# Two layers of Infini-attention and FFN: the order of each engine's operations as a written list of turns

## The chip, the cores and the metric

The kernel runs on one core of a Trainium2 chip. A core has five engines that each work through a list of instructions of their own: TensorE (PE) for matmuls, VectorE (DVE), ScalarE (ACT) and GpSimd (POOL) for everything elementwise, and SyncE (SP), which here only issues DMA transfers. Semaphores tie the lists together: an instruction can wait until another engine or a transfer has counted a semaphore up to a value. Matmul results land in PSUM, 8 banks of 512 floats for each of 128 partitions, and have to be moved from there to SBUF by DVE or ACT before the bank can be used again.

The metric is the device time of one execution in microseconds. The profile was taken from one execution of its own.

## The reference

The input x has 2048 tokens of 640 features, all in bf16. The stack is attention, FFN, attention, FFN, with the same weights for both rounds and a layer norm without parameters ahead of each part:

```python
x = x + A(layernorm(x), wq, wk, wv, wo, beta)
x = x + B(layernorm(x), w1, w2)      # relu(x @ w1) @ w2, 1728 hidden units
x = x + A(...)
x = x + B(...)
```

A is attention with a memory. 32 heads of 20 features work on 4 segments of 512 tokens. For every segment s and head:

```python
logits = qs @ ks.T * scale + mask            # causal, within the segment
a_dot  = softmax(logits) @ vs
a_mem  = (phi(qs) @ M) / (phi(qs) @ z + 1e-6)
o      = g * a_mem + (1 - g) * a_dot         # g = sigmoid(beta), one per head
M      = M + phi(ks).T @ vs                  # phi(t) = t + 1 if t > 0 else exp(t)
z      = z + phi(ks).sum(0)
```

The segments' outputs are put together and multiplied by wo.

## The kernel before

**Tiles and stages.** A segment of 512 tokens is the unit of all work, so there are 8 (round, segment) pairs. For each, four token tiles of 128 are normalised (DVE writes them to xn_tok, L704, or L716 in the first segment and in the FFN's norm), turned by a transposing DMA, and projected on PE: q and k with the features on the partitions (groups of 5 matmuls; the first of a group is recorded at L651, the others at L654), v with the tokens on the partitions. DVE or ACT moves each result out of its bank: q and k to the staging tile stg (DVE L827, ACT L828), v to v_aug, which has a column of ones for the denominators (DVE L878, ACT L879). q and k of two groups of 4 heads go through DRAM (scr) to pad, where each head begins at a multiple of 32 partitions, so that four heads' scores can be computed side by side in row tiles of PE (L1114, "rows"). ACT takes the exp of the scores into PT (L1166), POOL clears what lies above the diagonal (L1178), and PE multiplies by v in column tiles (L1257, "cols"), 16 matmuls with one evacuation to av (DVE L1265, ACT L1266); a DMA turns av to avt, and DVE divides by the sums (L1293, L1294, L1301). For two of the 32 pairs of head groups (all segments and rounds together) the product is formed by token instead, with the division straight from the bank (L1220, L1221, L1224).

The memory runs beside this: phi is a max (DVE L967), an exp (ACT L974) and a min (DVE L975); the update of M is PE L1058, the read PE L1007, always into the first of four banks, with its division on DVE (L1015, L1017, L1018), which frees that bank with L1018. The sum of both parts is turned and multiplied by wo, and DVE adds the result to x (L1328), which frees the bank and feeds the statistics of the next norm (L662, L664, L672). The FFN's first matmuls write hT (ACT L1436, DVE L1434), a last narrow part of the hidden units runs in column tiles (L1405), and its second matmuls are added to x at L1328 as well.

**Banks.** Four of the eight banks hold scores. The other four (MISC) are shared by all else that PE computes, so every evacuation by DVE or ACT sets when a later group of matmuls can start.

**What sets the order.** `plan()` describes the work as 33 streams, generators that yield one operation after another, each with the engines that may run it, a modelled duration, and the operations that it waits for. They are named by the order in which they are added: a is the scores, b the exps, d the products with v, h and i the projections by wo, j and k the FFN's norms, l and m the transfers to pad and scr, q and r the memory reads, y and z the projections to k and q, A that to v, B the FFN, E the constants (among them beta_bc), F the first loads. `Sched.run` simulates the engines: at each step it looks at the head of each stream, works out when it could start by the model, and takes the one with the earliest start, by priority where several tie. What it takes goes to the end of that engine's list. `keep_busy` puts small matmuls on the identity (L638) into PE's list where it expects a gap. SWITCH_NS, what it charges for a change of PE's mode, is varied over 48 values (STARTS), and of the 48 plans the one with the smallest sum of `late()` is taken, a replay of the plan with random delays of transfers. For these inputs that is the plan for 79.0. `Prog` leaves out waits that follow from earlier ones, and `emit` writes the lists.

So an operation's place in its engine's list is fixed when the kernel is built, and on the chip each engine works strictly in that order: an instruction that waits holds up all behind it on its engine.

## Time and profile before

| | |
|---|---|
| median of 3 runs | 562.49 us (562.12 to 563.04) |
| the profiled execution | 562.46 us |
| its span in the trace | 560.6 us |
| granted clock of PE | 1.00 |
| busy | PE 99%, DVE 73%, ACT 73%, POOL 35%; weight loads 54% |
| DMA engines, packets of queue 1 | 45.7% |

The span begins with the first instruction and ends with the last; the profiled execution's own time is 1.86 us longer. Lines such as L1265 are lines of the kernel before. In the timeline, consecutive instructions of one line on one engine are one row, with start and length in microseconds and their count behind the x; lengths of pipelined instructions overlap, so the distance between two starts tells more than the length. Square brackets at the end of a row hold idle time ahead of it and who ended it.

### The profile page before, as it was taken

Reading aid. Unit: us, or ns where it says so; the run is one execution under the profiler, and the core shown is the slowest. Engines: PE = TensorE matmul, PEld = TensorE weight load, DVE = VectorE, ACT = ScalarE, POOL = GpSimd, SP = SyncE. Lnnn points to the kernel's source line nnn. Section 1 sums busy time; section 2 is a strip of 40 time slices with the busy share of each in tenths; the row PEclk is TensorE's granted clock in tenths of the full one; section 3 lists DMA queues with packets and bytes.
Section 4 is the critical chain, followed back from the end, with each engine's and each line's share of the span. In section 5 each row is a group of like instructions: output and inputs, shape, how many; then the busy total and the mean of one; then the engine's idle time right before and its main releaser. Section 6 shows DMA issues by size and latency. Waiting matters only on the chain.

```text
span 560.6 us, 12651 instructions
## 1 busy us (share of the span) xinstructions
PE 555.5 (99%) x5110; PEld 302.6 (54%) x5111; DVE 410.8 (73%) x1060; ACT 409.7 (73%) x522; POOL 194.3 (35%) x302
## 2 busy tenths in 40 slices
...
DMA packets 132219, 61.43 MB, mean 110 GB/s; under 512 B 111042, under 2 KB 122050, under 8 KB 132162
## 3 DMA queue, kind: packets, MB, share of 16 engines
q1 hardware_dynamic: 131942, 60.37, 45.7%
...
q10 hardware_dynamic: 220, 0.26, 0.2%
q14 instruction: 17, 0.14, 0.1%
...
## 4 chain that ended last, share of the span: by engine, by line
PE 90%; DVE 8%; DMA 1%; ACT 0%; POOL 0%; issue 0%
PE ps L654 58%; PE ps L651 12%; PE ps L1114 9%; PE ps L1257 7%; DVE stats L662 2%; PE ps L1058 2%; PE ps L1007 2%; DVE x_sb L1328 1%; PE ps L1405 1%; DVE stg L827 1%; DMA x_sb<-in_A_x_dram 1%; DVE xn_tok L704 1%; DVE av L1265 0%; DVE xn_tok L716 0%; DVE mv L664 0%; ACT PT L1166 0%
## 5 line engine op out<-in xcount | busy, mean ns | idle before, releaser
L1166 ACT ACTIVATE PT<-ps 128x1024 bf16<-128x1024 f32 x320 | 310.1, 1022 | 66.1 <-PE ps L1114 64.5
L1178 POOL TENSOR_SCALAR_AFFINE_SELECT PT<-PT 128x512 bf16<-128x512 bf16 x256 | 166.3, 668 | 267.7 <-ACT PT L1166 267.7
L654 PE MATMUL ps<-w_r,hT 128*128 128x320 bf16 (+2 forms) x768 | 123.4, 299 | 0.1
L654 PE MATMUL ps<-xnT,w_r 128*128 128x512 bf16 x416 | 113.6, 379 | 0.0
L1328 DVE TENSOR_TENSOR x_sb<-x_sb,ps 128x320 bf16<-128x320 bf16 (+1 forms) x128 | 60.4, 479 | 70.2 <-PE ps L654 69.9
L654 PEld LDWEIGHTS ps<-w_r,hT 128*128 128x128 bf16 x768 | 72.2, 98 | 34.2 <-issue 6.3
L1436 ACT ACTIVATE hT<-ps 128x512 bf16<-128x512 f32 x55 | 33.0, 599 | 46.4 <-PE ps L654 46.1
L1114 PE MATMUL ps<-pad 20*128 20x384 bf16 (+3 forms) x1024 | 64.9, 301 | 0.0
L654 PEld LDWEIGHTS ps<-xnT,w_r 128*128 128x128 bf16 x416 | 39.7, 98 | 42.1 <-issue 2.9
L662 DVE BATCH_NORM_STATS2 stats<-x_sb 128x6 f32<-128x320 bf16 x126 | 55.9, 470 | 2.3 <-DMA x_sb<-in_A_x_dram 2.0
L1265 DVE CAST av<-ps 128x512 bf16<-128x512 f32 x56 | 38.3, 684 | 12.9 <-PE ps L1257 12.5
L1114 PEld LDWEIGHTS ps<-pad 20*128 20x128 bf16 x1024 | 18.2, 92 | 51.4 <-ACT PT L1166 24.2
L654 PE MATMUL ps<-wo_r,oT 128*128 128x320 bf16 x256 | 45.3, 299 | 0.0
L1434 DVE TENSOR_SCALAR hT<-ps 128x512 bf16<-128x512 f32 x49 | 33.5, 684 | 10.5 <-PE ps L654 10.0
L1257 PE MATMUL ps<-PT,v_aug 128*32 128x256 bf16 (+5 forms) x896 | 40.7, 302 | 0.0
L651 PE MATMUL ps<-xnT,w_r 128*128 128x512 bf16 x104 | 39.6, 381 | 0.0
L654 PE MATMUL ps<-wv_r,xnT 128*128 128x320 bf16 x192 | 35.8, 300 | 0.0
L654 PE MATMUL ps<-xnT,wk_r 128*128 128x512 bf16 (+1 forms) x140 | 35.5, 349 | 0.0
L676 POOL TENSOR_TENSOR rstd<-lnU,mhalf 128x2 f32<-128x2 f32 (+2 forms) x25 | 20.3, 811 | 39.9 <-DVE lnU L672 39.7
L654 PE MATMUL ps<-xnT,wq_r 128*128 128x512 bf16 (+1 forms) x140 | 33.9, 349 | 0.0
L1301 DVE TENSOR_TENSOR o_sb<-avt,rden 128x320 bf16<-128x320 bf16 x60 | 33.3, 572 | 0.7
L654 PEld LDWEIGHTS ps<-wo_r,oT 128*128 128x128 bf16 x256 | 24.8, 98 | 11.3 <-issue 1.3
...
## 6 DMA issues: line engine op xcount, KB each, us to landing
...
```

The lines of the kernel that those rows point to most:

```text
L651: bk, tk = yield pe(mm_ns(n), [(lambda e, bk, a=a, b=b: e.matmul(bk.ap[:, 0:n] if len(b.shape) == 2 else bk.ap[:, 0:n].rearrange("p (i n) ...
L654: tk = yield pe(mm_ns(n), [(lambda e, k=k, a=a, b=b, bk=bk: e.matmul(bk.ap[:, 0:n] if len(b.shape) == 2 else bk.ap[:, 0:n].rearrange("p (i ...
L662: tk = yield dve(320, 1, lambda e, c2=c2: e.bn_stats(stats6[:, t, c2, :], x_sb[:, t, c2 * 320:(c2 + 1) * 320]), xt)
L1114: fns.append([(lambda e, z=z, j=j, hh=hh, N=N, o=o, sl=sl: e.matmul(ps[:, hh, o:o + N], sl.ap[32 * hh:32 * hh + DH, z, 0, 128 * j:128 * j ...
L1166: tx = yield act(1024, lambda e, dst=dst, src=src: e.activation(dst, src, ACT.Exp, scale=SCALE), sc + pw)
L1178: tm = yield pool(600.0, lambda e, reg=reg: e.affine_select(out=reg, in_=reg, pattern=[[0, 4], [1, 128]], compare_op=ALU.is_ge, fill=0.0, ...
L1257: fns.append((lambda e, bk, j=j, hh=hh, pt=pt, g=g0 + z: e.matmul(bk.ap[32 * hh:32 * hh + wide(g, hh), 128 * j:L], VAUG[vx(a, s)][:, j].re ...
L1265: te = yield evac(L, 1, lambda e, sl=sl, z=z, bk=bk: e.tensor_copy(sl.ap[:, z], bk.ap), lambda e, sl=sl, z=z, bk=bk: e.activation(sl.ap[:, ...
L1301: to = yield dve(320, 1, lambda e, dst=dst, src=src, rz=rz: e.tensor_tensor(dst, src, rz, ALU.mult), [tg] + OSB.tks)
L1328: ta = yield dve(n, 1, lambda e: e.tensor_tensor(x_sb[:, t, c0:c0 + n], x_sb[:, t, c0:c0 + n], bk.ap[:, 0:n], ALU.add), [tk] + list(waits) ...
L1434: th = yield evac(512, 1, lambda e, dc=dc, bk=bk: e.tensor_scalar(hT[:, dc, :], bk.ap[:, :], 0.0, None, ALU.max), lambda e, dc=dc, bk=bk: ...
L1436: lambda e, dc=dc, bk=bk: e.activation(hT[:, dc, :], bk.ap[:, :], ACT.Relu), [tk] + HT.tks)
```

## The change

STARTS holds the single value 79.0, whose plan is the one that was taken before. `Sched` now also records each operation that it places. TURNS holds, for each of the five engines, a string with one letter per operation: the stream whose turn it is. `in_turns` builds a second `Prog` from the record: on each engine it takes the next operation of the stream named, so that a stream keeps its own order on that engine while streams pass each other, with the same engines, buffers and dependencies as in the plan, and works out anew which waits have to be written. That `Prog` is emitted. The letter H stands for the small matmuls of `keep_busy`.

On PE 2006 of 5113 operations stand at another place than before (by at most 40 places), on DVE 783 of 1062 (16), on ACT 92 of 526 (9), on SP 261 of 324 (15), on POOL 45 of 306. Lines in the new file are numbered 107 higher from `Sched`'s methods on, so that L1265 is L1372 there.

```diff
-STARTS = [SWITCH_NS + 0.75 * (k - 48 // 2) for k in range(48)]
+STARTS = [79.0]
...
+TURNS = {
+    "sp": (
+        "FFEFFFFFFFllllllmGmwwllllGmGGsGmllleGlllslGGGmGwwmemslGGGllmmGGGlllllslllllmGGggwwGllmmmmGGGelGljksG"
...
         self.log = []
+        self.record = []
...
+            fns = [(lambda e, ap=s.ap: self.idle_fn(e, ap), False)] * n
+            for fn, mark in fns:
+                self.P.op("pe", fn, mark)
+            self.record.append(("pe", len(self.streams), fns, None, s.tks, [], s, "full", 56.0 * n))
...
             self.log.append((e, hold, tail, waits, out if isinstance(out, list) else [out], op.dma is not None))
+            self.record.append((e, best[0][2], fns, op.dma, waits, out if isinstance(out, list) else [out], slot, op.mode, op.alts[k][1]))
...
+    def in_turns(self, turns):
+
+        names = "abcdefghijklmnopqrstuvwxyzABCDEFGHIJKLMNOPQRSTUVWXYZ"
+        todo = {e: {} for e in ENGS}
+        for r in self.record:
+            todo[r[0]].setdefault(names[r[1]], []).append(r)
+        seq = {e: [r for r in self.record if r[0] == e] for e in ENGS}
+        for e, order in turns.items():
+            assert sorted(order) == sorted(n for n, rs in todo[e].items() for _ in rs), e
+            its = {n: iter(rs) for n, rs in todo[e].items()}
+            seq[e] = [next(its[n]) for n in order]
+        P = Prog(self.P.clk)
...
+                    P.waits(e, [new[t] for t in waits])
+                    if sem is not None:
+                        got = [P.dma(e, fns[0][0], sem)]
+                    else:
+                        got = [t for t in [P.op(e, fn, mark) for fn, mark in fns] if t is not None]
...
+        P.waits("sp", [new[id(self.last[0]), self.last[1]]])
+        return P
...
-            S.P.emit(block)
+            S.in_turns(TURNS).emit(block)
```

Three places in the lists. The first is on DVE, at about 98 us of the trace, around the division of a memory read (rmem, om_sb) and the evacuation of a product with v (av). Before:

```order
L716 TENSOR_SCALAR xn_tok<-x_sb,mv,rstd 128x640 x2
L1015 TENSOR_SCALAR rmem<-ps 128x16
L975 TENSOR_TENSOR stg<-stg,rtmp 128x512
L967 TENSOR_SCALAR rtmp<-stg 128x512
L1017 RECIPROCAL rmem<-rmem 128x16
L1018 TENSOR_TENSOR om_sb<-ps,rmem 128x320
L1265 CAST av<-ps 128x512
```

After, at the same place on DVE:

```order
L1122 TENSOR_SCALAR rmem<-ps 128x16
L1124 RECIPROCAL rmem<-rmem 128x16
L1125 TENSOR_TENSOR om_sb<-ps,rmem 128x320
L1372 CAST av<-ps 128x512
L1082 TENSOR_TENSOR stg<-stg,rtmp 128x512
L1074 TENSOR_SCALAR rtmp<-stg 128x512
```

The min and the max of phi (stg, rtmp) moved behind the division and the evacuation.

The second is SP's list at the start: the loads of x, of the weights (wk_r, wq_r, wv_r) and of beta_bc, and the first transfers to pad. Before:

```order
L524 DMA x_sb<-in_A_x_dram 128x640
L518 DMA x_sb<-in_A_x_dram 128x2x640
L521 DMA wk_r<-in_A_wk_dram 128x5x256
L521 DMA wq_r<-in_A_wq_dram 128x5x256
L521 DMA wk_r<-in_A_wk_dram 128x5x384
L521 DMA wq_r<-in_A_wq_dram 128x5x384
L511 DMA wv_r<-in_A_wv_dram 128x5x640
L518 DMA x_sb<-in_A_x_dram 128x2x640 x2
L924 DMA pad<-stg 20x1024 x4
L610 DMA beta_bc<-in_A_beta_dram 128x32
```

After, on SP from the first row:

```order
L631 DMA x_sb<-in_A_x_dram 128x640
L625 DMA x_sb<-in_A_x_dram 128x2x640
L717 DMA beta_bc<-in_A_beta_dram 128x32
L628 DMA wk_r<-in_A_wk_dram 128x5x256
L628 DMA wq_r<-in_A_wq_dram 128x5x256
```

The load of beta_bc moved from behind the pads to the third place, and the other loads of weights follow in their old order.

The third is on DVE again, at about 314 to 318 us, where xn_tok is written for the next norm and results of wo are added to x_sb. Before:

```order
L704 TENSOR_SCALAR xn_tok<-x_sb,mv,rstd 128x640 x3
L1328 TENSOR_TENSOR x_sb<-x_sb,ps 128x320 x2
L704 TENSOR_SCALAR xn_tok<-x_sb,mv,rstd 128x640
L662 BN_STATS stats<-x_sb 128x6 x2
L1015 TENSOR_SCALAR rmem<-ps 128x16
```

After, at the same place on DVE:

```order
L811 TENSOR_SCALAR xn_tok<-x_sb,mv,rstd 128x640 x4
L1435 TENSOR_TENSOR x_sb<-x_sb,ps 128x320 x2
L1122 TENSOR_SCALAR rmem<-ps 128x16
L769 BN_STATS stats<-x_sb 128x6 x2
L1400 RECIPROCAL rden<-avt 128x32
```

The fourth write of xn_tok moved ahead of the two additions.

80 lines of the change are left out of this document (78 added, 2 removed).

## The prediction

> **What bounds the kernel now.** I read the page's first two lines, then the chain that ended last, then the timeline of PE, and last what the other engines do where PE stands still.
>
> ```profile
> span 560.6 us, 12651 instructions
> PE 555.5 (99%) x5110; PEld 302.6 (54%) x5111; DVE 410.8 (73%) x1060; ACT 409.7 (73%) x522; POOL 194.3 (35%) x302
> ```
>
> PE is busy for 555.5 of 560.6 us, so all idle time of PE together is 5.1 us, and some of that is the wait for the first data. A busy PE might still be slow, so the second question is its cadence. Three pieces of the chain (start, us, engine, line, count) show it where nothing disturbs:
>
> ```profile
> 489.15 1.76 PE ps L654 x13
> ...
> 504.63 0.86 PE ps L654 x4
> ```
>
> Thirteen matmuls of 320 columns take 1.76 us, 0.136 us each; four of 512 columns take 0.86, 0.216 each. In the timeline the durations of single matmuls overlap, so I work with starts: a stall is the distance between two starts less the count times this cadence. A change of order doesn't change these two numbers. It can only change the places where PE leaves the cadence, and there are two kinds.
>
> The first kind is a change of PE's mode (whole array, row tiles for the scores at L1114, column tiles for L1257 and L1405). The timeline (start, us, engine, line, operation, tiles, count) at one scores round:
>
> ```profile
> 128.66 0.57 PE L654 MATMUL ps<-w_r,hT 128*128 128x320 bf16 x3
> 129.16 0.40 PE L1114 MATMUL ps<-pad 20*128 20x512 bf16 x4
> 129.49 1.40 PE L654 MATMUL ps<-w_r,hT 128*128 128x320 bf16 x9
> ```
>
> Three matmuls should take 0.41, and the scores start after 0.50: 0.09 lost. Four scores matmuls lie side by side and should take 0.216; PE goes on after 0.33: 0.11 lost. So a change of mode costs 0.10. Counted along PE's list of operations there are 404 of them, some 40 us.
>
> The second kind is a wait. The largest of them, and what DVE did there:
>
> ```profile
> 99.20 0.71 PE L654 MATMUL ps<-wv_r,xnT 128*128 128x320 bf16 x4
> 99.87 0.34 PE L1007 MATMUL ps<-BD,w_r 128*128 128x147 bf16 x3
> 100.47 0.31 PE L651 MATMUL ps<-wv_r,xnT 128*128 128x320 bf16 x1 [0.25 <-DVE av L1265]
> ```
>
> ```profile
> 98.51 0.41 DVE L975 TENSOR_TENSOR stg<-stg,rtmp 128x512 bf16<-128x512 bf16 x1
> 98.84 0.28 DVE L967 TENSOR_SCALAR rtmp<-stg 128x512 bf16<-128x512 bf16 x1
> 99.04 0.24 DVE L1017 RECIPROCAL rmem<-rmem 128x16 f32<-128x16 f32 x1
> 99.32 0.49 DVE L1018 TENSOR_TENSOR om_sb<-ps,rmem 128x320 bf16<-128x320 f32 x1
> 99.73 0.68 DVE L1265 CAST av<-ps 128x512 bf16<-128x512 f32 x1
> ```
>
> The four matmuls from 99.20 end their turn at 99.74, but L1007 starts at 99.87, when L1018 has emptied the only bank that L1007 may use: 0.13. Its three matmuls take 0.19 (no wait is near them where I measured that), and L651 starts at 100.47 instead of 100.05, when L1265 has emptied its bank: 0.42. Together 0.54 us. Smaller ones stand at 58.86,
>
> ```profile
> 58.33 0.57 PE L654 MATMUL ps<-wv_r,hT 128*128 128x320 bf16 x3
> 58.86 0.84 PE L1058 MATMUL ps<-v_aug,phk 128*128 128x147 bf16 x10
> ```
>
> at 324.64,
>
> ```profile
> 324.17 0.38 PE L654 MATMUL ps<-xnT,w_r 128*128 128x512 bf16 x1
> 324.64 0.29 PE L638 MATMUL ps<-ident 128*128 128x128 bf16 x2
> ```
>
> and at 390.24:
>
> ```profile
> 389.99 0.30 PE L654 MATMUL ps<-w_u,hL 128*128 128x320 bf16 x1
> 390.24 0.34 PE L1007 MATMUL ps<-BD,stg 128*128 128x147 bf16 x3
> ```
>
> By the same reckoning 0.12 at 58.86 (0.53 less 0.41), 0.25 at 324.64 (0.47 less 0.22) and 0.11 at 390.24 (0.25 less 0.14). Two more, at 78.5 and 94.9, are about 0.10 each. This is nearly all that PE waits for once it has started: little more than 1.2 us can be won from waits.
>
> **The change, part by part.** Both kernels hold the same operations, buffers and choices of engine; the order in each engine's list is all that differs, with the waits that the order makes explicit.
>
> *Waits that go.* At 98.5 to 100.3 the new turns put L975 and L967 behind L1017, L1018 and L1265. From the starts above, these two take 0.53 us of DVE (98.51 to 99.04), so the bank of L1018 is free 0.53 earlier and that of L1265 as well: more than the 0.13 and the 0.42 that PE waits. Both stalls go: 0.54. At 58.86 the emptying of a bank (L1220, L1221, L1224) moves ahead of two multiplications L1301, each longer than the wait: 0.12. At 324.64 the release is this evacuation:
>
> ```profile
> 324.15 0.44 DVE L878 CAST v_aug<-ps 128x320 bf16<-128x320 f32 x1
> ```
>
> It moves ahead of three DVE operations, and the stall of 0.25 goes. The three of about 0.10 go likewise: 0.30. Sum of waits: 0.54 + 0.12 + 0.25 + 0.30 = 1.21 us. What is late next at these places is the matmul before, so nothing takes their place there.
>
> *Changes of mode.* The new PE list has 400 instead of 404: 4 x 0.10 = 0.40 us.
>
> *New waits on DVE.* This is the price I know least. PE owns few banks, so a DVE operation that moves ahead of an evacuation hands its own length to PE, as far as the margin doesn't cover it. The clearest case is here, first DVE and then PE:
>
> ```profile
> 315.29 0.87 DVE L1328 TENSOR_TENSOR x_sb<-x_sb,ps 128x320 bf16<-128x320 bf16 x2
> 316.09 0.43 DVE L704 TENSOR_SCALAR xn_tok<-x_sb,mv,rstd 128x640 bf16<-128x640 bf16 x1
> 316.44 0.87 DVE L662 BATCH_NORM_STATS2 stats<-x_sb 128x6 f32<-128x320 bf16 x2
> ```
>
> ```profile
> 316.02 0.30 PE L651 MATMUL ps<-wo_r,oT 128*128 128x320 bf16 x1
> ```
>
> L704 (316.09 to 316.44, so 0.35) now stands ahead of the pair L1328. The first of the pair ends in the middle, near 315.7, and frees the bank for the L651 at 316.02; 0.35 later is past 316.02 with what a wait needs, and I put PE's wait at 0.15. DVE can't make this up, since it has no gaps there. The stretch (length, then busy time of PE, PEld, DVE, ACT, POOL, PE clock, DMA share, GB/s):
>
> ```profile
> 310.00:327.00 17.00, 16.91 (x178) 9.20 (x176) 16.84 (x51) 13.65 (x16) 8.40 (x12) 1.00 0.39 83
> ```
>
> Comparing for each wait of PE on DVE how much work has moved ahead on DVE with the time to spare in the trace, I find 17 places where more was moved than was spare, the first and the last being the L651 of these two rows:
>
> ```profile
> 26.56 0.28 PE L651 MATMUL ps<-xnT,wq_r 128*128 128x256 bf16 x1
> ```
>
> ```profile
> 498.98 0.30 PE L651 MATMUL ps<-wo_r,oT 128*128 128x320 bf16 x1
> ```
>
> Of these I followed seven operation by operation. Five cost nothing, since DVE idles just before and the moved work falls into the gap; one costs 0.15, the one above, and one 0.10. So 0.25 for seven, 0.036 a place, and 17 x 0.036 = 0.6 us. The bounds: nothing, if all margins hold, and 0.35 (one L704) at half of the places, 9 x 0.35 = 3.15 us.
>
> *The start.* SP now issues the load of beta_bc third, ahead of all weights, instead of after the first pads. The two issues (start, us), the two transfers (KB, us to landing), the DMA engines' stretch, and the first use of wv:
>
> ```profile
> 4.63 2.12 SPq L511 DMA_DIRECT2D wv_r<-in_A_wv_dram  x1
> ...
> 17.52 0.49 SPq L610 DMA_DIRECT2D beta_bc<-in_A_beta_dram  x1
> ```
>
> ```profile
> wv_r<-in_A_wv_dram SPq DMA_DIRECT2D x1, 800.0 KB, 8.8
> ...
> beta_bc<-in_A_beta_dram SPq DMA_DIRECT2D x1, 8.0 KB, 2.6
> ```
>
> ```profile
> 2.00:13.00 11.00, 10.45 (x107) 9.40 (x106) 5.78 (x20) 5.69 (x13) 4.37 (x6) 1.00 1.04 330
> ```
>
> ```profile
> 14.07 0.30 PE L651 MATMUL ps<-wv_r,xnT 128*128 128x320 bf16 x1
> ```
>
> wv lands at 4.63 + 8.8 = 13.43 and is first used at 14.07; in the new PE list three matmuls of 256 columns (0.109 each, by the cadence of the others) fewer stand ahead, so it is wanted at 13.75, and 0.32 is to spare. If the queue is what counts, wv's issue slips by beta's 0.49 and PE waits 0.17. If the transfers count, for they are at their limit (share 1.04), 8 KB at 330 GB/s are 0.02 us and it's hidden. At worst all 2.6 us of beta's flight are added: 2.3 of wait. I take 0.1, between the two near ones. wk, wq and x are wanted at least two microseconds after they land. On DVE the small memset of the warm-up tile moves into the chain of the first layer norm:
>
> ```profile
> 1.77 0.06 DVE L580 MEMSET warm<- 128x1 f32 x1
> ```
>
> DVE works without a gap there until PE can start, so it costs its 0.06.
>
> *ACT, POOL and SP.* On ACT, 92 of 526 operations move; the largest single ones put an exp of phi ahead of a pair of softmax exps. It falls into time that ACT waits anyway (in total, times, longest), 0.58 us on average, as long as one such exp:
>
> ```profile
> ACT PT L1166 <- PE ps L1114: 64.5, 111, 2.4
> ```
>
> POOL is busy 35% of the time, and its 45 moved operations I put at nothing: the cover is its idle time. SP's later moves (transposes earlier, spills later) reach operations that are wanted a microsecond or more after they land; if that cover were gone, each would cost its delay, a few tenths.
>
> **The sum**, against the profiled execution (562.46, its span of 560.6 and 1.86 around it; the median of the runs is 562.49, the same within 0.03): 562.46 - 1.21 - 0.40 + 0.60 + 0.10 + 0.06 = 561.51, say 561.5 us.
>
> **The rivals.**
>
> All waits go and none comes: PE's new waits and wv's are hidden. 562.46 - 1.21 - 0.40 + 0.06 = 560.9. For it: five of seven places cost nothing. Against it: the stretch at 310 to 327, with DVE full.
>
> No net gain: the waits are exchanged. Ten of the 17 places at 0.15 make 1.5: 562.46 - 1.61 + 0.16 + 1.5 = 562.5.
>
> Slower, by DVE: PE is without slack, and each operation put ahead of an evacuation is paid in full: 9 places at 0.35 give 562.46 - 1.61 + 0.16 + 3.15 = 564.2. It decides from new waits of 1.45 us (four places at 0.35); over 0.2% slower it is from 2.57 (eight places). For it: DVE's 73%, in stretches 99%; against it, the places that I followed.
>
> Slower, by the start: the load of beta, 128 rows of 64 bytes, gets in the way of the weights for its whole flight, wv comes 2.6 later, PE waits 2.3: 562.46 - 1.61 + 0.06 + 0.60 + 2.3 = 563.8. The row that speaks for it is the share of 1.04; against it, its 8 KB are a hundredth of wv's. The Trainium skill, DMA: Bandwidth & Descriptors, Specifications, says that transfers under 512 bytes don't reach line rate, since they are done as read-modify-write, and that speaks against moving such a load ahead of the weights. Counted as 128 transfers of 512 bytes, 64 KB at the measured 330 GB/s, an estimate from that page, it would be 0.2 us, still inside wv's 0.32, so by the page the sum would lose its 0.1 and be 561.4. No row here shows such a load among the weights, so the trace neither agrees nor disagrees.
>
> **How the numbers follow.** The forecast has a chance of 0.42, all waits gone 0.14, no net gain 0.12, slower by DVE 0.26, slower by the start 0.06. The time is that of the forecast, 561.5, with a range of its own of 560.9 (no new waits) to 562.2 (new waits twice my 0.6). A measurement of this kernel tells about 0.2%, 1.12 us, from no change: faster is below 561.37, slower above 563.6. Of the forecast 0.26 lies below 561.37 and 0.16 within; with 0.14 of the first rival that's 0.40 faster. The exchange of waits gives 0.11 within and 0.01 above, so same is 0.27 and slower 0.26 + 0.06 + 0.01 = 0.33. The range reaches from 560.5 (the first rival with the changes of mode at twice their price) to 564.4 (the slower cases with a little more than nine places), and leaves some 0.2 outside.
>
> **What would show it.** Right: at about 99.3 L1007 starts at the cadence and no wait on L1265 follows; at 324 the two L638 start 0.22 after the matmul ahead; PE's idle total falls from 5.1 to near 4. A wait of PE on L1328 near 316 and a start of wv's first matmul near 13.8 to 13.9 would confirm the new prices. Wrong: a time above 563 with waits of PE on DVE spread over the first 300 us, or one large gap before 16 us; or the removed stalls still there, because a transfer or ACT was late just behind DVE.

## The result, and the profile after

The changed kernel takes 564.44 us (median of 6 runs, 563.76 to 564.66), the kernel before 562.47 us beside it (562.06 to 563.04). The ratio is 1.0032 with an interval of 1.0020 to 1.0044: slower by 0.32%, or 1.97 us, where 561.5 was forecast.

The head of the page of the kernel after:

```profile
span 561.6 us, 12640 instructions
PE 555.3 (99%) x5111; PEld 302.3 (54%) x5111; DVE 410.4 (73%) x1060; ACT 408.8 (73%) x522; POOL 192.1 (34%) x302
```

No engine has more work than before. The profiled execution of after took 563.76 us, its span 561.6, so 2.16 lie outside the span, where it had been 1.86. Its span is 1.0 longer than before's 560.6, with PE busy for 0.2 less.

**Where the time is.** Both kernels run the same matmuls, so one can ask when each has done the same amount of PE's work. This ledger is taken at places where both lists have done exactly the same matmuls. It holds the time at which a kernel gets there, less the column's time, at which the kernel before got there (in us from the span's start; one change of PE's mode more or fewer at the place makes 0.1):

| at | 12.8 | 17.9 | 34.6 | 52.7 | 108.1 | 162.8 | 188.5 | 255.0 | 387.4 | 551.3 |
|---|---|---|---|---|---|---|---|---|---|---|
| after | -0.19 | +0.18 | +0.77 | +0.77 | -0.01 | 0.00 | +1.14 | +1.34 | +1.22 | +0.99 |
| after, profiled again | -0.05 | +0.18 | +0.88 | +0.88 | +0.08 | +0.09 | +1.23 | +1.43 | +1.31 | +1.08 |

So the start wins 0.2, the stretch to 35 us loses about 1.0, the stretch from 53 to 108 wins 0.8, and the stretch from 163 to 188 loses 1.14. The rest nearly cancels. Both profiles come from executions near the lower end of their kernel's times; the part of after's median above 563.76 is looked at below.

**The waits that were to go.** PE's timeline of after near 59 us (start, us, engine, line, operation, tiles, count):

```profile
59.03 0.38 PE L761 MATMUL ps<-hT,wk_r 128*128 128x512 bf16 x1
59.24 0.77 PE L1165 MATMUL ps<-v_aug,phk 128*128 128x147 bf16 x9
```

The 512 columns take 0.21, the cadence: the stall ahead of L1165 (L1058 before) is gone, and so are those at 324, 390 and 95. At 78.5 there is 0.05 left. The largest one shrank but stayed. PE and then DVE of after, in the timeline:

```profile
99.26 0.30 PE L761 MATMUL ps<-wv_r,xnT 128*128 128x320 bf16 x1
99.74 0.34 PE L1114 MATMUL ps<-BD,w_r 128*128 128x147 bf16 x3 [0.18 <-DVE om_sb L1125]
```

```profile
98.71 0.16 DVE L1122 TENSOR_SCALAR rmem<-ps 128x16 f32<-128x16 f32 x1
98.90 0.25 DVE L1124 RECIPROCAL rmem<-rmem 128x16 f32<-128x16 f32 x1
99.19 0.49 DVE L1125 TENSOR_TENSOR om_sb<-ps,rmem 128x320 bf16<-128x320 f32 x1
```

The second wait (0.42, for av) is gone: the projection behind the read starts at 99.92, by the cadence. The first has grown from 0.13 to 0.34 (0.48 between the starts at 99.26 and 99.74, less 0.14). On DVE the division had begun earlier in the kernel before:

```profile
98.43 0.16 DVE L1015 TENSOR_SCALAR rmem<-ps 128x16 f32<-128x16 f32 x1
```

From there to the start of L1018 at 99.32 it took 0.89, two operations of phi included; in after it takes 0.48 (98.71 to 99.19), but begins 0.28 later. So the bank comes free only 0.13 earlier. And PE's new list has one matmul of the group ahead of L1114 (99.26) where four stood (99.20): it wants the bank at 99.40 instead of 99.74. 0.13 less 0.13, and 0.34 for what PE wants earlier.

One more wait went, which the list of stalls in the prediction doesn't hold. PE of the kernel before:

```profile
79.47 0.62 PE L638 MATMUL ps<-ident 128*128 128x128 bf16 x8
80.36 0.34 PE L1007 MATMUL ps<-BD,w_r 128*128 128x84 bf16 x3 [0.27 <-DVE om_sb L1018]
```

Eight matmuls at 0.057 take 0.46 and 0.89 passed, so 0.43 is a wait for the bank that om_sb (L1018) frees at 80.30. In after this read stands behind two more matmuls of the scores, starts at 81.11 and doesn't wait. This is more than half of what the stretch from 53 to 108 wins.

**The waits that came.** The largest is at 174 us. PE, then DVE, then ACT of after:

```profile
173.46 0.73 PE L1364 MATMUL ps<-PT,v_aug 128*32 128x512 bf16 x16
174.77 0.39 PE L758 MATMUL ps<-xnT,w_r 128*128 128x512 bf16 x1 [0.59 <-DVE hL L1517]
...
177.30 0.34 PE L1114 MATMUL ps<-BD,stg 128*128 128x147 bf16 x3 [0.30 <-DVE av L1372]
```

```profile
171.21 0.68 DVE L1372 CAST av<-ps 128x512 bf16<-128x512 f32 x1
171.81 0.83 DVE L1082 TENSOR_TENSOR stg<-stg,rtmp 128x512 bf16<-128x512 bf16 x1
172.56 1.22 DVE L811 TENSOR_SCALAR xn_tok<-x_sb,mv,rstd 128x640 bf16<-128x640 bf16 x2
173.70 0.28 DVE L1074 TENSOR_SCALAR rtmp<-stg 128x512 bf16<-128x512 bf16 x1
173.90 0.48 DVE L1408 TENSOR_TENSOR o_sb<-avt,rden 128x320 bf16<-128x320 bf16 x1
174.30 0.41 DVE L1517 TENSOR_SCALAR hL<-ps 128x256 bf16<-128x256 f32 x1
```

```profile
174.01 0.63 ACT L1081 ACTIVATE stg<-stg 128x512 bf16<-128x512 bf16 x1 [1.12 <-DVE rtmp L1074]
```

The same evacuation in DVE's timeline of the kernel before:

```profile
170.96 0.41 DVE L1410 TENSOR_SCALAR hL<-ps 128x256 bf16<-128x256 f32 x1
```

In after, the evacuation hL frees a bank at 174.7 instead of 171.4, since six operations stand ahead of it from 171.21 on, and PE's next group of matmuls waits for that bank: 0.66 over the cadence. The evacuation of av, five operations behind hL, costs another 0.37 at 177.30. ACT waits 1.12 for the max L1074, with the exps of the softmax queued behind.

The second place is near 26 us, PE and then DVE of after:

```profile
26.52 0.39 PE L761 MATMUL ps<-xnT,wk_r 128*128 128x256 bf16 x2
27.25 0.28 PE L758 MATMUL ps<-xnT,wq_r 128*128 128x256 bf16 x1 [0.34 <-DVE stg L934]
```

```profile
26.13 0.61 DVE L723 TENSOR_SCALAR gt<-gt 128x32 f32<-128x32 f32 x1
26.79 1.07 DVE L934 CAST stg<-ps 128x256 bf16<-128x256 f32 x3
```

The evacuations L934 come behind the four operations that make the gates from beta (L721 to L724, 25.39 to 26.79), and PE loses 0.50 (0.73 less two at 0.109). The third place is the start. SP's issue of wv, its flight (KB, us to landing) and PE:

```profile
6.00 1.08 SPq L618 DMA_DIRECT2D wv_r<-in_A_wv_dram  x1
```

```profile
wv_r<-in_A_wv_dram SPq DMA_DIRECT2D x1, 800.0 KB, 7.8
```

```profile
13.44 0.27 PE L761 MATMUL ps<-xnT,wq_r 128*128 128x256 bf16 x1
13.92 0.30 PE L758 MATMUL ps<-wv_r,xnT 128*128 128x320 bf16 x1 [0.21 <-ACT stg L935]
```

wv lands at 6.00 + 7.8 = 13.8; PE wanted it at 13.55 and starts at 13.92: 0.37 lost. The row names ACT, but the transfer is what ended last. PE's first projection, in turn, starts 0.2 earlier than before by the ledger.

The last is the wait near 316 that the prediction named:

```profile
316.50 1.03 PE L761 MATMUL ps<-xnT,w_r 128*128 128x512 bf16 x4
317.52 0.31 PE L758 MATMUL ps<-wo_r,oT 128*128 128x320 bf16 x1
```

Four matmuls of 512 columns take 0.86; 1.02 passed: 0.16. Two more of the same kind are 0.19 at 244.5 and 0.11 at 101.7.

All stalls of PE in after's trace add up to 3.0 us, in before's to 1.6, the 0.43 at 80 us among them. That is 1.4 more, less 0.3 for three changes of mode fewer and 0.2 for the earlier start, so 0.9, against the 1.0 by which the span grew.

### The profile page after: what moved, and what is told of

Read it like the earlier page. It is cut to its first block, busy times and chain, and to the rows that moved or that the text cites. A ratio compares the mean times of both kernels' runs of the same rounds, so it can differ in the third digit from the quotient of the medians.

```text
span 561.6 us, 12640 instructions
## 1 busy us (share of the span) xinstructions
PE 555.3 (99%) x5111; PEld 302.3 (54%) x5111; DVE 410.4 (73%) x1060; ACT 408.8 (73%) x522; POOL 192.1 (34%) x302
## 4 chain that ended last, share of the span: by engine, by line
PE 89%; DVE 9%; DMA 1%; POOL 0%; issue 0%; ACT 0%; SPq 0%
PE ps L761 57%; PE ps L758 12%; PE ps L1221 8%; PE ps L1364 6%; PE ps L1114 2%; DVE stats L769 1%; PE ps L1165 1%; DVE x_sb L1435 1%; DVE xn_tok L823 1%; PE ps L1512 1%; DVE xn_tok L811 1%; PE ps L1315 1%; DVE av L1372 1%; DMA x_sb<-in_A_x_dram 1%; DVE stg L1082 0%; PE ps L745 0%
## 5 line engine op out<-in xcount | busy, mean ns | idle before, releaser
L1372 DVE CAST av<-ps 128x512 bf16<-128x512 f32 x56 | 38.4, 686 | 18.3 <-PE ps L1364 18.0
L761 PE MATMUL ps<-wo_r,oT 128*128 128x320 bf16 x256 | 47.5, 299 | 0.0
L761 PE MATMUL ps<-wv_r,xnT 128*128 128x320 bf16 x192 | 37.4, 299 | 0.0
L934 DVE CAST stg<-ps 128x512 bf16<-128x512 f32 (+1 forms) x40 | 24.7, 623 | 13.5 <-PE ps L761 13.3
L1408 DVE TENSOR_TENSOR o_sb<-avt,rden 128x320 bf16<-128x320 bf16 x60 | 31.0, 534 | 0.5
```

What stands on the lines that cost most here:

```text
L761: tk = yield pe(mm_ns(n), [(lambda e, k=k, a=a, b=b, bk=bk: e.matmul(bk.ap[:, 0:n] if len(b.shape) == 2 else bk.ap[:, 0:n].rearrange("p (i ...
L1372: te = yield evac(L, 1, lambda e, sl=sl, z=z, bk=bk: e.tensor_copy(sl.ap[:, z], bk.ap), lambda e, sl=sl, z=z, bk=bk: e.activation(sl.ap[:, ...
L1408: to = yield dve(320, 1, lambda e, dst=dst, src=src, rz=rz: e.tensor_tensor(dst, src, rz, ALU.mult), [tg] + OSB.tks)
```

## Experiments

The theory after the result was this: PE loses where DVE comes late with an evacuation, in few places, above all near 174 and 26 us, and at the start for wv. The rivals were a shortage of DVE's time as such, SP's place for beta, and lists that fit only together. The times are medians; the kernel before ran on the same chip beside each (562.67 to 562.73).

### One engine's turns alone put back

DVE's list is put back to the order before, the other four stay new (the first of its eleven lines):

```diff
-        "EEuuuuuuEvuvuvuvvvuuvvvxowxwwwwwowowAwwwwwAAwwwwAoxEEEExxxoxxEExEEdoooAAAyAoEodAowwwwwotAwwwwwwAwwff"
+        "EEEuuuuuuvuvuvuvvvuuvvvoxowwxwwwwwwwwAwowwAAwwAwxwxEoEoExEEExEEExxxoodAAooAyAoodAwwowwwtAwwwtwAwwwwf"
...
```

> The changed kernel with the old turns on DVE alone; PE, SP, ACT and POOL keep the new ones. Theory (the loss comes from DVE operations put ahead of evacuations that PE waits for): the stalls of the new order at 26.6, 99.3, 173.9, 176.7, 244.5 and 317.1 (2.2 us together) go, the old one near 100 comes back (0.5), the fewer changes of PE's mode stay won (0.4), wv's 0.37 stays: 562.4 to 563.0. Rival (the loss comes from PE's own order, or from the start): 564 or more.

Measured: 581.01 us, ratio 1.0327 (1.0312 to 1.0341). PE's list is put back instead:

```diff
-        "DHuuHvvxxxxxxxxxxxxxxxxxxxxxxxxxxxxxxxxxxxxxAAAAxAAxAAxxxxxxxxxAAxAAxAAAAAAAAAAxxAAxxAAxxaAAAAxxxxAA"
+        "DHuuHvvxxxxxxxxxxxxxxxxxxxxxxxxxxxxxxxxxxxxxxxxxAAAAAxxxAAAAAxxAAAAAxxxxAAAAAxAAAAAxxxxxAAaAAAxxxAAAA"
...
```

> The changed kernel with the old turns on PE alone; all others keep the new ones. Theory (DVE's order makes the loss): the changes of mode come back (0.4), the stalls on DVE stay or grow, since the two lists no longer fit: 564.8 or more. Rival (PE's order makes the loss): 562.5 to 563.

Measured: 568.97 us, ratio 1.0108 (1.0094 to 1.0121). PE's timeline of the kernel with DVE's old list, at its largest gap:

```profile
455.94 0.62 PE L1221 MATMUL ps<-pad 20*128 20x512 bf16 x4 [3.95 <-ACT PT L1273]
```

Both sizes were far off what was expected. The largest gap waits for ACT, not for DVE; other waits of this kernel, of 0.2 to 1.5 us, are for DVE and for transfers: lists that are each a good order stop each other when one is exchanged. Behind the gap PE is also slower for a while:

```profile
457.26 3.41 PE L761 MATMUL ps<-w_r,hT 128*128 128x320 bf16 x12
```

These matmuls start 0.267 us apart, where 0.136 is their cadence elsewhere. The granted clock of the profile falls to 0.5 at 454.7, 2.7 us into the time in which PE is idle, and is back at 1.00 at 461.5, 5.5 us after PE goes on; in the rest of the run it is 1.00. So some 3 of the 17 us that this kernel loses against after are clock and not waiting (an estimate: half of the 5.5). None of the shorter waits is followed by a lower clock. An engine's whole list can't be judged alone, so the later runs either exchange a stretch of time on all engines or move a few neighbours.

### The start

SP's load of beta goes back behind the first pads, all else stays new:

```diff
-        "FFEFFFFFFFllllllmGmwwllllGmGGsGmllleGlllslGGGmGwwmemslGGGllmmGGGlllllslllllmGGggwwGllmmmmGGGelGljksG"
+        "FFFFFFFFFllllEllmGmwwllllGmGGsGmllleGlllslGGGmGwwmemslGGGllmmGGGlllllslllllmGGggwwGllmmmmGGGelGljksG"
```

> The changed kernel with one letter of SP's turns back where it was: the load of beta_bc stands again behind the first pads instead of third, ahead of the weights. The trace of the changed kernel has wv landing at 13.79 (before: 13.43) and PE's first wv matmul waiting at 13.44 for 0.37 us; it also has the first tile of x landing 0.26 us earlier and PE's first projection 0.20 us earlier. Theory (the small load delays wv): the wait of 0.37 goes, time 564.1. Rival 1 (the small load also lets the first x land earlier, since the weights start later): the wait goes, but PE starts 0.20 later, time 564.3. Rival 2 (wv is late for another reason): wait stays, 564.4.

Measured: 563.94 us, ratio 1.0023 (1.0014 to 1.0031). PE doesn't wait for wv any more: it is issued at 4.59, lands at 12.95 and is used at 13.78. But the first x lands at 3.80 instead of 3.51, the first projection starts at 9.74 instead of 9.51, and a stall of 0.22 stands at 15.63. Over all traces x lands first at 3.51 to 3.98 with beta third (10 traces, median 3.62) and at 3.66 to 3.84 with beta behind the pads (9 traces, median 3.79). So part of what beta's place costs at wv it wins at x; the 0.34 by which this kernel's median lies below that of after's second set (564.28, below) is within the two intervals.

The same letter alone is moved in the kernel before, whose order is written as turns for this:

```diff
-        "FFFFFFFFFllllEllmGmwwllllmGGGmsllllllllesGGGGGmGwwmGemsllllmmGllllsGGGGGGmGllllGmmGGmggwwllllsmGjekl"
+        "FFEFFFFFFFllllllmGmwwllllmGGGmsllllllllesGGGGGmGwwmGemsllllmmGllllsGGGGGGmGllllGmmGGmggwwllllsmGjekl"
```

> The kernel before with one move: SP loads beta_bc third, ahead of the weights. Theory (from the traces of the changed kernel, with and without that move): the first tile of x lands 0.2 earlier and PE's first projection starts 0.2 earlier; wv lands some 0.35 later, near 13.8, which is 0.2 less than PE's need; together within 0.2 us of before. Rival (the small load costs PE a wait for wv here too, or a later pad): 0.3 to 0.6 slower.

Measured: 562.74 us, ratio 1.0001 (0.9992 to 1.0009). SP's timeline, wv's flight and PE:

```profile
5.26 1.60 SPq L618 DMA_DIRECT2D wv_r<-in_A_wv_dram  x1
```

```profile
wv_r<-in_A_wv_dram SPq DMA_DIRECT2D x1, 800.0 KB, 8.2
```

```profile
13.95 0.30 PE L758 MATMUL ps<-wv_r,xnT 128*128 128x320 bf16 x1
```

wv lands at 13.46 and is wanted at 13.95: in the order before, beta's place costs nothing. The new order costs 0.37 at this point because it moved beta ahead of wv and also wants wv 0.4 earlier (13.55).

### Evacuations near the places that wait

Seven evacuations on DVE are moved ahead of what the change had put before them (two of L934 at 26 us, hL at 174 and 244.5, av at 176.6 and two additions to x_sb at 316.6). The pieces of DVE's list at 26 and 172 us, as - and + of after and of this kernel:

```diff
-        "EEuuuuuuEvuvuvuvvvuuvvvxowxwwwwwowowAwwwwwAAwwwwAoxEEEExxxoxxEExEEdoooAAAyAoEodAowwwwwotAwwwwwwAwwff"
+        "EEuuuuuuEvuvuvuvvvuuvvvxowxwwwwwowowAwwwwwAAwwwwAoxxEExEExoxxEExEEdoooAAAyAoEodAowwwwwotAwwwwwwAwwff"
...
-        "CBpnBdqqqAyqqqABqoqfqfAofqfqnqdAydAAyffffnBBrrrdBrrrBrrridrhririhjjijjjhkjhkjdkkkkkojffzkzofjdfBnooB"
+        "fBdpnBqqqAyqqqABqoqfqfAofqfqnqdAydAAyffffnBBrrrdBrrrBrrridrhririhjjijjjhkjhkjdkkkkkojffzkzofjdfBnooB"
...
```

(C, the evacuation hL, has moved to the line ahead, before the last two letters w, which write xn_tok.)

> The changed kernel with seven evacuations moved ahead on DVE by one to four places, and nothing else: at 26.6 two copies of k and q ahead of the small work on beta's gates, at 174 the evacuation into hL ahead of two writes of xn_tok, a max of phi and a division, at 176.6 that into av ahead of a min, an addition and one into hT, at 244.5 that into hL ahead of the third write of xn_tok, at 316.6 the two additions to x ahead of the fourth. Theory: each stall of PE there goes, 0.50 + 0.66 + 0.37 + 0.19 + 0.16 = 1.9 us, time 562.6. Rival (DVE is full there, so what is let pass makes PE wait a little later): less than half of it, 563.6 or more.

Measured: 564.29 us, ratio 1.0026 (1.0016 to 1.0037), no better than after. All the stalls aimed at are gone. What took their place, ACT, then PE of this kernel:

```profile
174.65 0.63 ACT L1081 ACTIVATE stg<-stg 128x512 bf16<-128x512 bf16 x1 [1.47 <-DVE rtmp L1074]
```

```profile
33.04 0.39 PE L1221 MATMUL ps<-pad 20*128 20x512 bf16 x4 [0.59 <-DMA pad<-scr]
...
177.16 0.40 PE L1221 MATMUL ps<-pad 20*128 20x256 bf16 x8 [0.67 <-ACT PT L1273]
```

The max L1074 is 0.63 later than in after (174.33 for 173.70), ACT waits 1.47 for it, the exps behind come late, and the scores' banks with them: 0.73 lost at 177.16. At 32 us what was won at 26 is lost again to the transfers to pad, 0.66. A third new stall, 0.51 at 326.37, waits for an evacuation of v_aug that ends at 326.31; after has none there. So near 174 two things are late on DVE: an evacuation for PE, and a max for ACT.

The next kernel starts from after again and moves only DVE's operations at 172 to 177 us: hL, the max too, and av ahead of the last phi and hT operations:

```diff
-        "dBBwwBffffnnBwwwrrrBdwrBrwrihdjwrihjrirjjhrirjkwrjhktkkdkkjktjjpzBkktffffdppnBwwwppzfBpfwpBfwwdpwwpf"
-        "CBpnBdqqqAyqqqABqoqfqfAofqfqnqdAydAAyffffnBBrrrdBrrrBrrridrhririhjjijjjhkjhkjdkkkkkojffzkzofjdfBnooB"
+        "dBBwwBffffnnBwwwrrrBdwrBrwrihdjwrihjrirjjhrirjkwrjhktkkdkkjktjjpzBkktffffdppnBwwwppzfBpfwpBfwwdpCpww"
+        "fBdpnBqqqAyqqqABqoqfqfAofqfqnqdAydAAyffffnBBrrrdBrrrBrrridrhririhjjijjjhkjhkjdkkkkkojffzkzofjdfBnooB"
```

> The changed kernel with three operations moved on DVE at 172 to 177 us: the evacuation into hL and the max of phi (L1074) ahead of the two writes of xn_tok, and the evacuation into av ahead of a min, an addition and one into hT. In the run with seven evacuations moved, PE's stalls of 0.66 and 0.37 there went, but the scores then waited 0.73 for ACT's exp, which stood behind an exp of phi, which waited 1.47 for this max. Theory (the late max on DVE is the cause, by way of ACT): the loss of 1.2 us between 173 and 178 goes but for some 0.2, the time falls by 1.0. Rival (DVE is simply full there): less than 0.4 is won.

Measured: 564.59 us, ratio 1.0035 (1.0023 to 1.0048). The stalls at 174 and 177.3 are gone, and one of 1.17 at 178.2 has come. DVE and PE of this kernel:

```profile
176.55 0.91 DVE L1426 TENSOR_TENSOR o_sb<-o_sb,om_sb 128x640 bf16<-128x640 bf16 x1
177.38 0.68 DVE L1541 TENSOR_SCALAR hT<-ps 128x512 bf16<-128x512 f32 x1
```

```profile
178.21 0.30 PE L758 MATMUL ps<-wv_r,xnT 128*128 128x320 bf16 x1 [1.03 <-DVE rmem L1122]
```

The row names rmem (L1122), which needs no bank of this group; what ended just before is the evacuation of hT at 178.06, which now stands behind av and the 0.91 of L1426.

Is it the amount of DVE's work? In the next kernel two multiplications of one division (162.3 us) write 16 elements of a row instead of 320, and one addition of om_sb to o_sb (164.1) writes 32 instead of 640. It leaves the other columns uncomputed, so its output isn't that of the reference; the order is that of after.

```diff
+            if m == 8:
+                dst, src, rz = dst[:, :, :, 0:1], src[:, :, :, 0:1], rd.ap[:, NJ * z:NJ * z + NJ]
...
+                if (a, s, g) == (0, 2, 0):
+                    dst, src = dst[:, :, 0:8], src[:, :, 0:8]
```

> The changed kernel, with three operations of DVE cut to a few columns: the two multiplications of one division at 161.9 and 162.3 us and the addition of the memory's part at 164.3. Most of the columns they should write keep old values; nothing else is left out. That takes some 1.6 us from DVE, 8 to 12 us ahead of the place where PE stalls for 0.66 and 0.37 us, and the operations right ahead of the late evacuations stay as they are. Theory (DVE is full from 155 to 178, and PE waits for whatever DVE gets to last): PE's loss between 160 and 180 shrinks by 0.8 to 1.2, time 563.4. Rival (only what stands right ahead of an evacuation counts): less than 0.3 is won.

Measured: 563.96 us, ratio 1.0021 (1.0013 to 1.0030). From 163 to 188 us it loses 1.11, as after does (1.14). DVE of this kernel:

```profile
167.86 0.35 DVE L1400 RECIPROCAL rden<-avt 128x32 f32<-128x32 bf16 x1 [0.65 <-DMA avt<-av]
...
174.71 0.41 DVE L1521 TENSOR_SCALAR hL<-ps 128x256 bf16<-128x256 f32 x1
```

The edit takes 0.87 us (0.62 and 0.25) from DVE, not the 1.6 expected. They turn into waits, 0.20 for PE at 164.46 and 0.65 for the transposing transfer of av, and hL comes as late as in after. So a little less work ahead of this place doesn't help; that it is the order, the next kernel tests.

Last, eleven operations of DVE between 171 and 177 us are ordered by who is waiting: hL (PE), the min and the max of phi (ACT), then xn_tok, then hT and av, the divisions last.

```diff
-        "dBBwwBffffnnBwwwrrrBdwrBrwrihdjwrihjrirjjhrirjkwrjhktkkdkkjktjjpzBkktffffdppnBwwwppzfBpfwpBfwwdpwwpf"
-        "CBpnBdqqqAyqqqABqoqfqfAofqfqnqdAydAAyffffnBBrrrdBrrrBrrridrhririhjjijjjhkjhkjdkkkkkojffzkzofjdfBnooB"
+        "dBBwwBffffnnBwwwrrrBdwrBrwrihdjwrihjrirjjhrirjkwrjhktkkdkkjktjjpzBkktffffdppnBwwwppzfBpfwpBfwwdCppww"
+        "BpdBfnqqqAyqqqABqoqfqfAofqfqnqdAydAAyffffnBBrrrdBrrrBrrridrhririhjjijjjhkjhkjdkkkkkojffzkzofjdfBnooB"
```

> The changed kernel with twelve operations of DVE between 171 and 177 us in the order in which they are needed: evacuation to hL, min and max of phi, the two writes of xn_tok, evacuation to hT, min, evacuation to av, evacuation to hT, and only then the division and the addition of the memory's part, which nothing waits for soon. Theory (the order on DVE makes the loss there, and the two earlier edits put another needed operation last): PE's stalls of 0.66 and 0.37 go but for 0.2, ACT isn't held up, the span falls from 562.1 to 561.3. Rival (DVE can't do what is needed in time in any order): less than 0.3 is won, with a new wait of PE or ACT near 176.

Measured: 563.30 us, ratio 1.0012 (1.0003 to 1.0020), and a median span of 561.1 where after has 562.1 to 562.25. PE of this kernel:

```profile
173.87 0.73 PE L1364 MATMUL ps<-PT,v_aug 128*32 128x512 bf16 x16
174.53 0.39 PE L758 MATMUL ps<-xnT,w_r 128*128 128x512 bf16 x1
...
178.18 0.39 PE L758 MATMUL ps<-xnT,wk_r 128*128 128x512 bf16 x1 [0.25 <-DMA xnT<-xn_tok]
```

The stall at 174 is gone. What is left, 0.41 at 177.8, is the transposing transfer of xn_tok, whose writes now come later on DVE. By the times and the spans 1.0 us is won. By the ledger this stretch loses 0.53 instead of 1.14, so 0.6 is shown to come from it; where the other 0.4 is won, this one trace doesn't show. Eleven neighbours on one engine are worth a third to a half of what the whole change lost.

### Stretches of the old order on all engines

In the following kernels a stretch of the run has the old turns on all five engines and the rest the new ones, with the seam at a place where both lists have done the same operations. DVE's second line shows it for the first kernel, old up to 52 us and new from there; behind the seam (from the 16th letter on) the lines agree:

```diff
-        "tdwwywopwtoyffdzoozApAopotfdddofAfftppAoywAopdpddoyozwypwopwwwwwddowwwpdwywzwpdddzrrrzwowrrrowdrrorh"
+        "fpofdywwowwtyfdzoozApAopotfdddofAfftppAoywAopdpddoyozwypwopwwwwwddowwwpdwywzwpdddzrrrzwowrrrowdrrorh"
```

> All five engines keep the old turns until about 52 us and take the new ones from there. The traces of before and of the changed kernel, compared at the same amount of PE work, have the changed one 0.75 us behind at 52 us. Theory (the lists of a stretch belong together, and the losses of the stretches add up): the 0.75 are saved, 0.7 us below the changed kernel, 1.2 us above the kernel before. Rival (what is late in the first 50 us is made good later anyway, or the seam costs a wait): within 0.3 us of the changed kernel.

Then the new turns from 52 to 160 alone. Its first seam is the same; the second, near 160, is in DVE's fourth line, and all lines behind are the old ones:

```diff
-        "dBBwwBffffnnBwwwrrrBdwrBrwrihdjwrihjrirjjhrirjkwrjhktkkdkkjktjjpzBkktffffdppnBwwwppzfBpfwpBfwwdpwwpf"
+        "dBBwwBffffnnBwwwrrrBdwrBrwrihdjwrihjrirjjhrirjkwrjhktkkdkkjktjjptfzBkkffdfnppzBwwpwpBwfBppdwwfwCwppf"
...
```

> The new turns on all engines from 52 to 160 us alone, where the stalls of the kernel before at 58.9, 78.5, 94.9 and 100 lie; the old ones before and after. Theory (the stalls there do go, and nothing later takes them back): 0.97 us faster than the kernel before. Rival (what PE wins is lost in the next wait for a transfer or for ACT): within 0.3 us of before.

And from 52 to 160 and from 200 us on, with a third seam in the fifth line, behind which the new order goes on:

```diff
-        "CBpnBdqqqAyqqqABqoqfqfAofqfqnqdAydAAyffffnBBrrrdBrrrBrrridrhririhjjijjjhkjhkjdkkkkkojffzkzofjdfBnooB"
+        "BfBndpqqqAyqoqABqfqoqAffqfqndqAydAAyffffBnBrrrdBrrrBrrridrhririhjjijjjhkjhkjdkkkkkojffzkzofjdfBnooB"
```

> The old turns on all engines until 52 us and from 160 to 200 us, the new ones from 52 to 160 and after 200. Compared at the same PE work, the new turns lose 0.75 us until 52, win 0.97 from 52 to 160, lose 1.35 from 160 to 200 and win 0.14 after that. Theory (the parts add up): 1.1 us faster than the kernel before. Rival (seams and later waits eat it): not faster than before by more than 0.3.

Then the new turns only from 52 to 125; the second seam is in DVE's third line:

```diff
-        "hoijjohhpprijrjijArjikkjdkkkpkjqjkpqqAkkqqqdppqyfAqqffqqqAppfdttttffpBdffnBnqqqdqqqBqqqBBqfffBBqfqdB"
+        "hoijjohhpprijrjijArjikkjdkkkpkjqjkpqqAkkqqqdppqyfAqqffqqqAppfdttttffpBdffnBnqqqdqqqBqqqBBBfqfqfBqBfd"
...
```

> The new turns on all engines from 52 to 125 us alone, the old ones before and after, those from 150 to 178 among them. Until 110 the new turns win 0.75 us for PE. Theory (DVE has no time to spare from 150 to 178, where the trace of before has it busy for 10.00 of 10 us; PE can come there no earlier than DVE's work lets it): the 0.75 are lost again between 150 and 180, the span is that of before within 0.3, 560.5 to 561.1. Rival (in the earlier runs the order of the new turns near 160 took the gain back, not DVE's load): the gain is kept, span 560.05, the fastest of all kernels.

Then from 52 to 125 and from 200 on, put together from the seams shown:

> The old turns on all engines until 52 and from 125 to 200 us, the new ones from 52 to 125 and after 200. Theory (stretches add up): -0.7 from 52 to 125 as in the run with new turns there alone, -0.1 to -0.2 after 200: span 560.0, against 560.9 of before. Rival (the lead that PE wins is lost at the new order's waits after 200, at 244, 317 and 390): 560.6 or more.

And old turns only from 125 to 200, that is the two middle seams without the first:

```diff
-        "dBBwwBffffnnBwwwrrrBdwrBrwrihdjwrihjrirjjhrirjkwrjhktkkdkkjktjjpzBkktffffdppnBwwwppzfBpfwpBfwwdpwwpf"
+        "nBdBwwwBffffnBwwwdrBrrrrBriwhwdrjihrjirjjihrjrjkhrjkwtkkdjjktkpktfzBkkffdfnppzBwwpwpBwfBppdwwfwCwppf"
...
```

> The changed kernel with the old turns on all engines from 125 to 200 us. Theory (the new lists of that stretch lose 1.0 to 1.35 us, whatever came before): the span falls from 562.1 to 561.0. Rival (the old turns there only hold when PE comes as early or late as in the kernel before; with what the first 50 us left behind they lose as well): 561.8 or more.

| new turns | us | ratio to before | interval | median span |
|---|---|---|---|---|
| from 52 on | 564.67 | 1.0039 | 1.0026 to 1.0053 | 562.8 |
| 52 to 160, from 200 on | 563.40 | 1.0016 | 1.0008 to 1.0025 | 561.5 |
| 52 to 160 | 563.41 | 1.0014 | 1.0005 to 1.0023 | 561.2 |
| 52 to 125 | 562.35 | 0.9993 | 0.9984 to 1.0002 | 560.2 |
| 52 to 125, from 200 on | 562.40 | 0.9996 | 0.9987 to 1.0005 | 560.5 |
| all but 125 to 200 | 564.42 | 1.0039 | 1.0024 to 1.0054 | 562.3 |

The kernel before has a median span of 560.8 to 560.9. The ledger of their profiled executions:

| new turns | 34.6 | 52.7 | 108.1 | 162.8 | 188.5 | 255.0 | 387.4 | 551.3 |
|---|---|---|---|---|---|---|---|---|
| from 52 on | 0.00 | +0.01 | -0.79 | -0.78 | -0.02 | +0.18 | +0.40 | +0.84 |
| 52 to 160, from 200 on | -0.04 | -0.03 | -0.83 | -0.50 | +0.05 | +0.36 | +0.30 | +0.83 |
| 52 to 160 | +0.03 | +0.03 | -0.69 | -0.36 | +0.28 | +0.28 | +0.27 | +0.15 |
| 52 to 125, from 200 on | +0.08 | +0.08 | -0.66 | -0.66 | -0.66 | -0.46 | -0.52 | -0.07 |
| all but 125 to 200 | +1.55 | +1.55 | +0.75 | +0.75 | +0.75 | +0.95 | +0.88 | +1.11 |

(The profiled execution of the kernel with 52 to 125 alone had an extra stall of 0.70 at 58.4 and a longer time than the median; its ledger isn't used.)

What follows. (The expectations above count a win of 0.97 from 52 to 160 and a loss of 1.35 from 160 to 200, from a coarser ledger; at places with exactly the same matmuls done they are 0.77 and 1.14.) The old turns up to 52 us take the early loss away every time: 0.08 or less at 34.6, against 0.77 to 1.55 in six profiles whose first 52 us are those of after, with a mean of 1.15. That mean is 0.4 above the 0.77 of after's first profile, which would account for most of the 0.65 by which after's median span stands above that profile's.

What sets the early loss is the last of the four transfers from scr to the pads, which PE needs for its first scores. SP's issue of them in after, and in before:

```profile
26.69 2.68 SPq L1052 DMA_DIRECT2D pad<-scr  x4
```

```profile
26.98 1.58 SPq L945 DMA_DIRECT2D pad<-scr  x4
```

In before the last one lands at 31.53 and PE starts these scores at 31.83, so 0.30 is to spare. In all eight profiles whose lists up to 35 us are those of after or differ from them only by beta's place or by the two evacuations at 26 us, the last one lands at 32.69 (after) to 33.47, PE starts 0.05 behind it, and the loss at 34.6 is that landing less 31.92, within 0.01. So the stalls for wv and at 26 us run beside this wait, and taking one of them away, as two of the kernels did, leaves it. The transposing transfers from xn_tok to hT, ahead of these four, land at 28.67 and 29.91 in after, at 27.76 and 28.89 in before; why the issue of the four takes so much longer, no run shows.

The new turns from 53 to 108 win 0.72 to 0.80 each time. The loss of 1.14 between 163 and 188 is gone in both kernels with old turns from 125 to 200 (-0.66 stays -0.66, +0.75 stays +0.75). But the last kernel is not faster than after: its early loss was the largest, and 0.34 was lost in it near 390. And the first kernel, without the early loss, is not faster either: it loses 0.86 between 188 and 551, where after, with the same turns, wins 0.15. Most of that lies near 390, where the four kernels with a seam and new turns behind 200 us lose 0.34 to 0.64 between 387 and 392 and after wins 0.12. DVE and PE of the first kernel:

```profile
388.54 0.35 DVE L1400 RECIPROCAL rden<-avt 128x32 f32<-128x32 bf16 x1 [0.83 <-DMA avt<-av]
```

```profile
390.97 0.38 PE L758 MATMUL ps<-xnT,w_r 128*128 128x512 bf16 x1 [0.27 <-DVE x_sb L1435]
```

DVE waits for the transposing transfer of av, so the addition to x_sb that PE waits for comes late; in after DVE doesn't wait there. An early gain isn't always kept by the later stretches, and this is the place where it was lost; why av's transfer doesn't come earlier when PE does, these profiles don't show.

With the seam at 160 the gain is lost around it. The theory that this comes of DVE's load would have it lost with the seam at 125, too; it is kept there, so the order between 125 and 160 is the likelier cause. DVE and PE of the kernel with new turns from 52 to 160, and DVE of the kernel before:

```profile
155.72 0.28 DVE L779 TENSOR_SCALAR lnU<-mv 128x2 f32<-128x2 f32 x2
```

```profile
165.65 0.38 PE L758 MATMUL ps<-xnT,w_r 128*128 128x512 bf16 x1 [0.59 <-DMA xnT<-xn_tok]
```

```profile
153.48 0.16 DVE L672 TENSOR_SCALAR lnU<-mv 128x2 f32<-128x2 f32 x1
```

The norm's small step lnU, on which the chain over POOL to rstd and xn_tok hangs, moved from 153.48 to 155.72, and PE waits at 165.65 for the transposed xn_tok. The operation takes 0.16 of DVE, so its place two microseconds later, and not its length, would be the cause; no run moves it alone to show it.

### The kernel after once more

The kernel after without an edit, in a set of its own beside the kernel before:

> The changed kernel again, for a second trace and for times on the chip of the other runs. The profiled execution was 0.7 us faster than the median. Expected 564.4; where this trace is slower than the first, the difference shows at waits that depend on transfers (the pads near 32 us, wv near 13.5), if the theory holds that the new turns leave these less to spare; the rival is a difference spread evenly.

Measured: 564.28 us (9 runs, 563.68 to 565.54), ratio 1.0029 (1.0020 to 1.0039). Its ledger stands in the first table and agrees with after's within 0.15 everywhere.

### What is better than both

The new turns win from 52 us on, and by 112 us they have won all that they win. So: new turns from 52 to 112, old ones elsewhere. The second seam in DVE's third line:

```diff
-        "hoijjohhpprijrjijArjikkjdkkkpkjqjkpqqAkkqqqdppqyfAqqffqqqAppfdttttffpBdffnBnqqqdqqqBqqqBBqfffBBqfqdB"
+        "hoijjohhpprijrjijArjikkjdkkkpkjqjkpqqAkkqqqdppqyfAqqffqqqAppfdttttffpBdffnnBqqqdqBqqBqqBqBfqfqfBqBfd"
...
```

> The new turns on all engines from 52 to 112 us alone, the old ones before and after. Theory: as with new turns from 52 to 125, PE gains 0.7 us there and keeps them; span 560.1 to 560.2 against 560.9 of before, and the time in all 562.0 to 562.4, depending on the time outside the span, which was 1.86 or 2.15 in the kernels so far and which nothing in the traces explains. Rival: the seam costs a wait, span 560.6 or more.

Measured: 562.02 us, ratio 0.9990 (0.9981 to 0.9999), median span 559.9. In its trace the wait of 0.34 at 99 us is still there, so the division of the memory read goes ahead of the second write of xn_tok:

```diff
-        "hoijjohhpprijrjijArjikkjdkkkpkjqjkpqqAkkqqqdppqyfAqqffqqqAppfdttttffpBdffnnBqqqdqBqqBqqBqBfqfqfBqBfd"
+        "hoijjohhpprijrjijArjikkjdkkkpkjqjkpqqAkqqqkdppqyfAqqffqqqAppfdttttffpBdffnnBqqqdqBqqBqqBqBfqfqfBqBfd"
```

> As the kernel with new turns from 52 to 112 us, and on DVE at 98 to 100 us the three operations of the memory's division moved ahead of the second write of xn_tok. Theory (DVE's order makes PE's wait of 0.34 at 99.4; the write is not wanted before 105): 0.3 us less than that kernel, span 559.8. Rival (the write's transfer comes too late then, or the division waits in any case): no gain against it.

Measured: 561.89 us, ratio 0.9987 (0.9978 to 0.9996), median span 559.7. PE and DVE of this kernel:

```profile
98.96 0.30 PE L761 MATMUL ps<-wv_r,xnT 128*128 128x320 bf16 x1
99.09 0.33 PE L1114 MATMUL ps<-BD,w_r 128*128 128x147 bf16 x3
```

```profile
98.21 0.49 DVE L1125 TENSOR_TENSOR om_sb<-ps,rmem 128x320 bf16<-128x320 f32 x1
```

L1114 starts at the cadence and the wait is gone, so it can go. In this profile 0.23 at 58.5 and 0.14 at 51.5 came elsewhere, and the 0.13 us between this kernel and the one without the moved division can't be told from none. Against the kernel before the change it is faster by 0.13%, 0.84 us: small, with an interval that leaves out 1.

## Why the prediction was wrong

*Waits that go (1.21).* Mostly right. The stalls at 58.9, 324.6, 390.2 and 94.9 went, and half of the one at 78.5. At 99 to 100 us 0.34 of the 0.54 stayed. The step took the bank to come free 0.53 earlier, and PE to want it when it had; it came free 0.13 earlier, and PE's own new turns want it 0.34 earlier. So about 0.85 of the 1.21 came true. The last kernel shows that the rest was to be had. The list was called nearly all that PE waits for, and it left out the 0.43 at 80.36, which went too, unforeseen.

*Changes of mode (0.40).* About right: by the traces' weight loads PE changes its mode 401 times in before and 398 times in after, three fewer at 0.09 to 0.10 each, so 0.3.

*New waits on DVE (0.60).* This is the step that failed. The place it named, near 316, came as predicted (0.15 forecast, 0.16 measured). The others were priced at the mean of seven that had been followed. In the trace DVE's new waits are 0.66, 0.50, 0.37, 0.19, 0.16 and 0.11, which makes 2.0, more than three times the 0.60. The first of the 17 places, near 26 us, alone cost 0.50, though the wait for the pads runs beside it. Places aren't alike: one with six operations in front of it costs 0.66, eighteen times the mean of 0.036, so a mean over a few that were followed says nothing of the rest. The rival that put the operations' lengths on PE in full gave 564.2 and was the nearer one, but by other numbers, few places at up to 0.66 and not nine at 0.35.

With the measured terms the sum is 562.46 - 0.85 - 0.43 - 0.30 + 2.0 + 0.37 for wv - 0.2 for the earlier start + 0.3 outside the span = 563.35, and the profiled execution took 563.76. The 0.4 that is left lies in places of under 0.1 each and in the roughness of the terms. The forecast's own terms add up to 561.61 and not to 561.51, which changes nothing in the account.

*The start (0.16).* 0.10 for wv was a choice between 0 and 0.17, with 2.3 as the worst case; in after's profile it was 0.37, in the other profiles with its first 52 us between 0.12 and 0.77, except for the second profile of after, which has none. Moving beta back shows that this is beta's place; moving it forward in the kernel before shows that it needs the new PE list as well, which the step had seen (it took wv's spare time down from 0.64 to 0.32). Missed was that x lands earlier, which pays 0.2 of it back; so the rival of a slower start, with 2.3 for wv, falls.

*ACT, POOL and SP (nothing).* Wrong for ACT: the cover was called the time that ACT waits anyway, but what it waits for near 174 is DVE's max, and the wait of 1.12 (1.47 with the evacuations first) holds the softmax's exps. Wrong for SP as well, and this is the second step that failed: its transfers were called wanted a microsecond or more after they land, but the last transfer to the first pads had 0.30 to spare in before. It lands at 31.53 there and at 32.69 to 33.47 with the new list, and sets the early loss of 0.77 to 1.55.

*The forecast and its range.* 561.5 was a gain of 1.0; it was a loss of 1.97, and the range ended at 564.4, 0.04 below the median. That the range nearly reached it is luck: its end stood on nine places at 0.35 each and a little more, which isn't what came. Summed by stretches, with the mean of six profiles for the first one, it is 0.30 outside the span, 1.15 up to 35 us, -0.78 to 108, 1.15 to 188 and -0.15 behind: 1.67. The 0.3 that is left to 1.97 lies in executions that have no profile.

*What stays open.* Why more time lies outside the span of after, 2.16 instead of 1.86, isn't seen in any trace. It is steady per kernel: 1.76 to 1.88 in the kernel before and seven of the others, 2.14 to 2.18 in after and nine others, which differ in little but order. One count goes with it: DVE's list has 16 separate wait instructions in every kernel of the second group and 17 or 18 in every kernel of the first, but no run changes that alone. Open, too, is why the last transfer to the first pads lands later with the new list, and up to 0.8 apart between executions.
